# First layer of the last two token blocks by seven block products

## The chip, the cores and the metric

The kernel runs on one core of a Trainium2 chip. The time is device microseconds (us) of one execution. Six parts of the core appear below: TensorE (PE) multiplies matrices into PSUM banks, VectorE (DVE) and ScalarE (ACT) do everything between two products, GpSimd (POOL) only clears a few tiles at the start, SyncE (SP) puts transfers into DMA queues, and the DMA engines move data between DRAM and the core's SBUF.

## What is computed

Attention in chunks (4 batches, 8 heads, 768 tokens, head dimension 64) gives 3072 tokens of 512 features, and two feed-forward networks follow:

```python
x = attention(q, k, v, mem_k, mem_v)       # 24 chunks of 32 per sequence; keys: 8 memory, 16 left, 32 own, 8 right
h = x @ w_in                               # (3072, 512) @ (512, 2048): "first layer"
g = np.maximum(0.01 * h, h)
y = g @ w_out                              # (3072, 2048) @ (2048, 512): "second layer"
a, b = y @ w_a, y @ w_b                    # (3072, 512) @ (512, 1536), twice: "third layer"
out = (a * b) @ w_out2                     # (3072, 1536) @ (1536, 512)
```

Every float32 operand X is used as two parts, X = hi + lo (hi is a rounding to the type float32r, lo the rest), and a product W·X becomes three matmuls: lo·hi + hi·lo + hi·hi.

## The kernel before

**Blocks.** The tokens are six blocks of 512 (`TB`), numbered 0 to 5. Attention is done in 24 units of 128 tokens, four to a block. A unit is a short pipeline: `a_scores` (32 small matmuls on TensorE), `a_soft1` and `a_soft2` (maximum, difference, exponential, sum, division: VectorE and one ScalarE operation), `a_turn` (16 transposes of 32 rows on VectorE, in block 0 on TensorE), `a_pv` (32 small matmuls), and `a_out` (ScalarE makes the hi part of x, VectorE the lo part).

**Items.** The first two layers run as items (bi, f): block bi, feature tile f of 16. An item is `mm1` (4 groups of 3 matmuls of 512 columns into a PSUM bank of `ps_h`; then ScalarE makes g and gh, VectorE gl) and `mm2` of the item two places back (`LAG`), 12 matmuls of 512 columns into the four banks `acc` of the block (`ps_a`). The attention unit of block bi+1 is spread over the items of block bi: scores at item f, softmax at f+1, transposes at f+2, values at f+3, with f = 2, 5, 8, 11 in blocks 1 to 4. So block 4 carries the attention of block 5, and block 5 carries none. When `mm2` has done f = 15, ScalarE copies the four banks into tiles `x2` (tag `z`, three buffers), and a DMA writes each to the scratch tensor `x2d`.

**Preparation.** The weights of the third layer and of the last one are made ready by `prep_steps`: 18 groups of 4 steps. Steps one and two each join a raw weight tile (ACT one operation, DVE two), step three splits the plain blocks and makes four differences, step four splits those; the results go to DRAM. The loop over items takes 72 steps over the 64 items of blocks 1 to 4.

**The third layer** takes two blocks of 512 tokens at a time (`NS` = 3 pairs) as a 2 by 2 block product done with seven products in place of eight: `xc_make` builds the seven right-hand sides from the two x blocks with four subtractions (`t1` to `t4`), `layer3` runs the seven products.

**Order.** Tile's planner puts each engine's instructions in order by program position and by what its costs say is ready. `InOrder` is a wrapper around an engine: while `on` is true, each instruction that it emits is held behind the one that it emitted before on that engine, so the order is that of the program. It is on in the first items and from the third layer on; in the items between it is off, and the planner may run preparation ahead of its place.

**Queues.** Loads and stores are issued by SP, one after another: weights of the second layer (`wo_load`, tag `wo`, six buffers), attention inputs (`q_load`, `k_load`, `v_load`), raw weights, preparation's results, `x2d`, and `xs_load` (the x blocks of the third layer).

Of the kernel before, what the change touches and what calls it, by code (L numbers as in the profile page):

```python
# [14 lines left out]
P = 128  # L15
# [12 lines left out]
NB3 = NT // TB  # L28

# [24 lines left out]
def kernel(  # L54
# [74 lines left out]
    class Weights:  # L129
# [66 lines left out]

    att = tc.tile_pool(name="att", bufs=4, side="left")
# [4 lines left out]
        ap_.tile([P, 2 * CH, 16], F32, tag=t, name="qs", bufs=1) for t in ("pz", "ps", "pwa", "pwb")  # L202
# [18 lines left out]
    kt, vt, st, qr = {}, {}, {}, {}  # L221

    loaded = [0, 0, 0]

    def q_load(upto):
        while loaded[0] < min(upto, NU):
            u = loaded[0]
            if u < len(qs):
                eng = act if u < 1 else sp
                sp.dma_start(out=qs[u][0:64, 0:CH, :], in_=q_l[u, 0:64])  # L230
                eng.dma_start(out=qs[u][64:128, CH:2 * CH, :], in_=q_l[u, 64:128])
            else:
                t = ap_.tile([P, CH, 16], F32, tag="qr", name="qr", bufs=2)
                sp.dma_start(out=t, in_=q_l[u])
# [14 lines left out]
    def k_load(upto):  # L249
        while loaded[1] < min(upto, 2 * NU):  # L250
            u, cp = divmod(loaded[1], 2)
            t = ap_.tile([P, 512], F32, tag="k", name="k")
            sp.dma_start(out=t, in_=k_l[u, cp])
# [137 lines left out]
    x1 = {}  # L391

# [167 lines left out]
    for bi in range(1, NB3):  # L560
# [112 lines left out]
    def prep_steps():  # L676
        n = 0
        for p in range(NF2 // 2):
            for m in range(3):
# [17 lines left out]
                def plain(c, n, src):  # L697
                    w_parts(
                        wa[:, c:c + n, 0], wa[:, c:c + n, 1],
                        src.rearrange("p (a n) -> p a n", n=256), nc.vector,  # L700
                    )

                def plain4(c, src):
                    w_parts(*[
                        wa[:, c, l].rearrange("p (d a j) -> p d a j", d=2, j=32) for l in range(2)
                    ], src, nc.vector)

                def comb(c, x, y, op):
# [7 lines left out]
                    nc.vector.tensor_tensor(out=o, in0=x, in1=y, op=op)  # L716
# [25 lines left out]
                w_parts(wb[:, :, 0], wb[:, :, 1], t, nc.vector)  # L742
# [618 lines left out]
```

## Time and profile before

| | us |
|---|---|
| median of 3 runs | 1129.55 |
| lowest and highest | 1129.17, 1130.9 |
| the profiled execution | 1128.36 |
| its span, first to last instruction | 1126.5 |

The profile holds one execution. Its span is 1.9 us shorter than its time. Busy time of TensorE is that of pipelined matmuls whose ends are modelled: a matmul of 512 columns is listed with 389 ns, but the next one starts 227 ns after it, and the second number is what it costs in a row of them. The same holds in a smaller measure for VectorE and ScalarE, where independent operations overlap by some 80 to 100 ns.

### The profile page before, as it was taken

To read this page: it belongs to the slowest core of one execution; us is meant where nothing else is said; L and a number is where in the kernel's file an instruction comes from. 1 tells how busy PE (TensorE), PEld (TensorE's weight loads), DVE (VectorE), ACT (ScalarE), POOL (GpSimd) and SP (SyncE) were. 2 spreads that over 40 slices of the span, in tenths; PEclk is the share of its full clock that TensorE was granted. 3 is DMA by queue.
4 is the path that set the end of the run, shared out by engine and by line. 5 is a ranking of instruction groups with operands and counts; after the bars stand their busy time and mean duration, and the time that the engine had idled before them with its cause. 6 is when DMAs were issued, how large, how long until landed. Compare 5 with 4: busy or idle time off the path is not lost.

```text
span 1126.5 us, 16314 instructions
## 1 busy us (share of the span) xinstructions
PE 1108.6 (98%) x6242; PEld 919.2 (82%) x6242; DVE 726.6 (64%) x1334; ACT 499.4 (44%) x846; POOL 6.3 (1%) x16
## 2 busy tenths in 40 slices
PE   7899999999999999999999999999999999999997
PEld 6788888888888888888888888888888888888886
DVE  6796488778958873646111636578745679745666
ACT  5887555456555543425222434243434243343232
POOL 2000000000000000000000000000000000000000
PEclk9999999999999999999999999999999999999999
DMA  9996799999999985425445857566867576757452
GB/s 319 396 345 229 288 313 333 322 333 332 330 315 337 332 319 186 150 81 203 142 155 170 301 174 213 169 211 201 271 222 235 154 239 187 238 177 243 145 188 74
DMA packets 98509, 269.57 MB, mean 239 GB/s; under 512 B 9600, under 2 KB 23040, under 8 KB 97664
## 3 DMA queue, kind: packets, MB, share of 16 engines
q1 hardware_dynamic: 97264, 267.88, 71.0%
q8 instruction: 49, 0.80, 0.3%
q10 hardware_dynamic: 1168, 0.66, 0.2%
q14 instruction: 28, 0.23, 0.1%
HBM read 214.50 MB, written 54.00 MB: 238 GB/s over the span
## 4 chain that ended last, share of the span: by engine, by line
PE 97%; ACT 1%; DVE 1%; DMA 0%; SPq 0%; issue 0%; DVEq 0%
PE ca L47 18%; PE cc L47 9%; PE oa L47 8%; PE h L410 8%; PE a L530 8%; PE a L533 8%; PE a L534 8%; PE h L411 8%; PE h L412 8%; PE cb L47 5%; PE oy L47 4%; PE pv L383 2%; PE s L274 2%; PE oz L47 1%; ACT p L47 0%; DMA k<-kl 0%
## 5 line engine op out<-in xcount | busy, mean ns | idle before, releaser
L47 PE MATMUL ca<-ch,wab 128*128 128x512 f32 x575 | 191.8, 389 | 0.0
L410 PE MATMUL h<-xh,w 128*128 128x512 f32 (+1 forms) x384 | 151.5, 394 | 0.7 <-ACT xh L47 0.7
L530 PE MATMUL a<-gh,w 128*128 128x512 f32 (+1 forms) x392 | 150.6, 384 | 0.0
L533 PE MATMUL a<-gl,w 128*128 128x512 f32 (+1 forms) x392 | 150.4, 384 | 0.0
L534 PE MATMUL a<-gh,w 128*128 128x512 f32 (+1 forms) x392 | 150.4, 384 | 0.0
L411 PE MATMUL h<-xl,w 128*128 128x512 f32 (+1 forms) x384 | 148.5, 387 | 0.2 <-DVE xl L47 0.2
L412 PE MATMUL h<-xh,w 128*128 128x512 f32 (+1 forms) x384 | 148.4, 387 | 0.0
L508 DVE TENSOR_TENSOR gl<-g,gh 128x512 fp32r<-128x512 f32 (+1 forms) x96 | 65.3, 680 | 104.8 <-ACT gh L505 100.9
L47 ACT CAST st<-gb 128x512 fp32r<-128x512 f32 x126 | 76.5, 621 | 124.6 <-DVE gb L47 124.0
L47 PEld LDWEIGHTS ca<-ch,wab 128*128 128x128 f32 x575 | 107.9, 188 | 22.8
L502 ACT ACTIVATE g<-h 128x512 f32<-128x512 f32 (+1 forms) x96 | 56.3, 587 | 128.1 <-PE h L412 127.4
L47 PE MATMUL ca<-cl,wab 128*128 128x512 f32 x288 | 112.1, 389 | 0.0
L47 PE MATMUL oa<-st,wt 128*128 128x512 f32 x420 | 104.3, 389 | 0.0
L47 PE MATMUL cc<-ch,wab 128*128 128x512 f32 x288 | 100.4, 389 | 0.0
L47 DVE TENSOR_TENSOR st<-gb,st 128x512 fp32r<-128x512 f32 x126 | 85.3, 689 | 14.9 <-ACT st L47 13.2
L47 PEld LDWEIGHTS oa<-st,wt 128*128 128x128 f32 x420 | 78.8, 188 | 16.4
L530 PEld LDWEIGHTS a<-gh,w 128*128 128x128 f32 x392 | 73.7, 188 | 15.1 <-ACT x L547 0.4
L533 PEld LDWEIGHTS a<-gl,w 128*128 128x128 f32 x392 | 73.7, 188 | 14.5
L534 PEld LDWEIGHTS a<-gh,w 128*128 128x128 f32 x392 | 73.6, 188 | 14.5
L410 PEld LDWEIGHTS h<-xh,w 128*128 128x128 f32 x384 | 72.1, 188 | 16.3 <-ACT xh L47 0.8
L412 PEld LDWEIGHTS h<-xh,w 128*128 128x128 f32 x384 | 72.1, 188 | 14.7
L411 PEld LDWEIGHTS h<-xl,w 128*128 128x128 f32 x384 | 72.2, 188 | 14.2 <-DVE xl L47 0.5
(150 smaller groups left out, 1620.4 us busy)
## 6 DMA issues: line engine op xcount, KB each, us to landing
wab<-wab SPq DMA_DIRECT2D x126, 512.0 KB, 4.4
w<-wod SPq DMA_DIRECT2D x80, 512.0 KB, 5.0
raw<-w SPq DMA_DIRECT2D x68, 512.0 KB, 6.9
wt<-wtd SPq DMA_DIRECT2D x63, 512.0 KB, 4.5
k<-kl SPq DMA_DIRECT2D x48, 256.0 KB, 5.5
v<-vl SPq DMA_DIRECT2D x48, 256.0 KB, 5.2
wab<-pwb SPq DMA_DIRECT2D x12, 768.0 KB, 6.9
wod<-w SPq DMA_DIRECT2D x16, 512.0 KB, 6.3
```

The source lines that it names most:

```text
L47: self.last = emit(*args, **kwargs).ins
L274: pe.matmul(s[64 * cpar:64 * cpar + 64, cp * 4 + hp, :], qb[:, o, :], k[:, r:r + 64], start=True, stop=True,)
L383: pe.matmul(o[64 * hpar:64 * hpar + 64, 2 * pair:2 * pair + 2, t0:t0 + CH], v[:, i:i + 64], pt[:, 2 * cp + pair, 2 * cpar + hpar].rearrang ...
L410: pe.matmul(ps, w[1], x[0], start=first, stop=False)
L411: pe.matmul(ps, w[0], x[1], start=False, stop=False)
L412: pe.matmul(ps, w[0], x[0], start=False, stop=last)
L502: act.activation(g[:, c], ps[:, c], AF.Prelu, alpha=0.01)
L508: dve.tensor_tensor(out=gl[:, c], in0=g[:, c], in1=gh[:, c].bitcast(F32), op=ALU.subtract)
L530: pe.matmul(ps, slot[:, 1, c], gh[:, t], start=f == 0 and o == 0, stop=False, **kw)
L533: pe.matmul(ps, slot[:, 0, c], gl[:, t], start=False, stop=False, **kw)
L534: pe.matmul(ps, slot[:, 0, c], gh[:, t], start=False, stop=f == NF1 - 1 or (o == HALF and f == LEAD - 1), **kw)
```

## The change

Blocks 4 and 5 no longer run as items of their own. The first layer of both together is done as a 2 by 2 block product with seven products, per pair of feature tiles.

- **Attention.** 16 units (8 to 23) now lie beside the 48 items of blocks 1 to 3, started at the items in `STARTS`, two or three items apart instead of three, and five or more at a block's start; the last one starts at item 59 and its values come at item 62 of 63. `SEQ` puts unit 16 ahead of unit 12. Units of blocks 4 and 5 are written by `a_raw` as plain float32 into the tiles `xr` (ScalarE copy, no VectorE work); the first two go through DRAM (`x4d`), since the tile is not free yet.
- **Preparation.** 58 of the 72 steps lie in blocks 1 to 3. The other 14 lie in the new loop, two per pair.
- **Right-hand sides.** After block 3's items, `y_part` and `y_sub` build the seven right-hand sides Y from `xr`, with seven casts on ScalarE and eleven operations of 1024 columns on VectorE.
- **Seven products.** For each of 8 pairs of feature tiles, `s_sums` and `s_parts` build the four sums of W_in blocks, `prod` runs seven products of six matmuls, `snapped` and `summed` combine them, and `relu` makes g. The products of the second layer for block 4 run between them; the g of block 5 is kept in the freed W_in tiles (`kept`).
- **Output products of block 5** run last, 16 times 12 matmuls, in banks of `ps_h` and `ps_s`. `xs_load(0)` and `xc_make(0)` move there.
- `InOrder` is switched on ahead of `y_part(0)` for TensorE, VectorE and ScalarE, and stays on.

```diff
+NL = NB3 - 2
+SEQ = list(range(12)) + [16, 12, 13, 14, 15] + list(range(17, NU))
...
-                    raw = ap_.tile([P, 512, 2], I32, tag="raw", name="raw", bufs=4)
+                    raw = prep.tile([P, 512, 2], I32, tag="raw", name="raw", bufs=4)
...
+    prep_pool = tc.tile_pool(name="prep", bufs=1, side="left")
+    prep = prep_pool.__enter__()
...
+    qu, ku, vu = [[a[u] for u in SEQ] for a in (q_l, k_l, v_l)]
...
+    xr, x4d = {}, {}
+    def a_raw(u):
+        blk, k = divmod(SEQ[u], TB // UT)
+        o = pvt.pop(u)
+        c = slice(k * UT, k * UT + UT)
+        if blk in xr:
+            act.copy(xr[blk][:, :, c], o)
+            return
+        t = tp.tile([P, KC, UT], F32, tag="t", name="x4")
+        act.copy(t, o)
+        x4d[k] = dp.tile([P, KC, UT], F32, tag=f"x4d{k}", name=f"x4d{k}")
+        sp.dma_start(out=x4d[k], in_=t)
+    def x_raw():
+        for h, tag in enumerate(("xh", "xl")):
+            xr[NL + h] = xp.tile([P, KC, TB], F32, tag=tag, name="xr")
+        for k in x4d:
+            sp.dma_start(out=xr[NL][:, :, k * UT:k * UT + UT], in_=x4d[k])
...
-            acc[bi] = [ps_a.tile([P, TB], F32, tag="a", name="a") for _ in range(KC)]
+            last = bi == NB3 - 1
+            acc[bi] = [
+                p.tile([P, TB], F32, tag=t, name="a")
+                for p, t in (((ps_h, "h"), (ps_s, "s")) * 2 if last else ((ps_a, "a"),) * KC)
+            ]
...
-    for bi in range(1, NB3):
+    for bi in range(1, NL):
...
-    for bi in range(NB3 - 1):
-        for k, f in enumerate([5, 8, 11, 14] if bi == 0 else [2, 5, 8, 11]):
-            u = (bi + 1) * (TB // UT) + k
-            at(bi, f, a_scores, u)
-            at(bi, f, load_qk, u)
-            at(bi, f, a_soft1, u)
-            at(bi, f + 1, a_soft2, u)
-            if bi == 0:
-                at(bi, f + 2, a_turn_pe, u, ps_s, "s")
-            else:
-                at(bi, f + 2, a_turn, u)
-            at(bi, f + 3, a_pv, u, ps_s, "s")
-            at(bi, f + 3, load_v, u)
-            at(bi, f + 3, a_out, u, ("x", bi + 1), k * UT)
-    prep = ap_
+    for k, f in enumerate([5, 8, 11, 14]):
+        u = TB // UT + k
+        at(0, f, a_scores, u)
+        at(0, f, load_qk, u)
+        at(0, f, a_soft1, u)
+        at(0, f + 1, a_soft2, u)
+        at(0, f + 2, a_turn_pe, u, ps_s, "s")
+        at(0, f + 3, a_pv, u, ps_s, "s")
+        at(0, f + 3, load_v, u)
+        at(0, f + 3, a_out, u, ("x", 1), k * UT)
+    def at_item(i, *args):
+        at(*divmod(i, NF1), *args)
+    STARTS = (17, 20, 23, 26, 29, 32, 34, 37, 40, 42, 45, 48, 50, 53, 56, 59)
+    for k, i in enumerate(STARTS):
+        u = 2 * TB // UT + k
+        blk, o = divmod(SEQ[u], TB // UT)
+        at_item(i, a_scores, u)
+        at_item(i, load_qk, u)
+        at_item(i, a_soft1, u)
+        at_item(i + 1, a_soft2, u)
+        at_item(i + 2, a_turn, u)
+        at_item(i + 3, a_pv, u, ps_s, "s")
+        at_item(i + 3, load_v, u)
+        if blk < NL:
+            at_item(i + 3, a_out, u, ("x", blk), o * UT)
+        else:
+            at_item(i + 3, a_raw, u)
...
+    STEPS = 58
     for bi, f, parts in items[LEAD:]:
-        first, last = bi == 0, bi == NB3 - 1
-        if last and f == 0:
-            for _ in steps:
-                pass
-            att.__exit__(None, None, None)
-            xq = ctx.enter_context(
-                tc.tile_pool(name="xq", bufs=1, side="left", reuse_waits="tile")
-            )
-        if f == 0 and not last and not first:
-            x_tiles(("x", bi + 1))
+        first = bi == 0
+        if f == 0 and not first:
+            if bi + 1 < NL:
+                x_tiles(("x", bi + 1))
+            else:
+                x_raw()
...
-            for _ in range(72 * (i + 1) // 64 - 72 * i // 64):
+            n = (NL - 1) * NF1
+            for _ in range(STEPS * (i + 1) // n - STEPS * i // n):
...
+    att.__exit__(None, None, None)
+    xa_pool = tc.tile_pool(name="xa", bufs=1, side="left", reuse_waits="tile")
+    xa = xa_pool.__enter__()
+    ya, hc, homes = {}, KC // 2, {}
+    two = "p k n -> p (k n)"
+    def y_home(i, l):
+        if i in (0, 1, 3):
+            return xa.tile([P, hc, TB], F32R, tag=f"y{i}{l}", name="y")
+        if i == 2:
+            return wop.tile([P, hc, TB], F32R, tag="wo", name="y")
+        if i == 6:
+            key, tag, h = 6, "xh", l
+        else:
+            key, tag, h = l, ("xh", "xl")[l], i - 4
+        if key not in homes:
+            homes[key] = xp.tile([P, 2, hc, TB], F32R, tag=tag, name="y")
+        return homes[key][:, h]
+    def y_part(i):
+        t = Y[i].rearrange(two)
+        hi, lo = [y_home(i, l) for l in range(2)]
+        ya[i] = hi, lo
+        hi, lo = hi.rearrange(two), lo.rearrange(two)
+        act.copy(hi, t)
+        dve.tensor_tensor(out=lo, in0=t, in1=hi.bitcast(F32), op=ALU.subtract)
+    b11, b21, b12, b22 = [
+        xr[NL + h][:, k * hc:k * hc + hc] for h in range(2) for k in range(2)
+    ]
+    Y = (b11, b21, b21, b12, b12, b11, b22)
+    def y_sub(out, x, y):
+        dve.tensor_tensor(out=out, in0=x, in1=y, op=ALU.subtract)
+    sums_, sw = {}, {}
+    def s_sums(p):
+        zs = []
+        for f in (2 * p, 2 * p + 1):
+            w = wslot[f, 0]
+            z = tp.tile([P, 512], F32, tag="z", name="zs", bufs=3)
+            dve.tensor_tensor(out=z, in0=w[:, 0].bitcast(F32), in1=w[:, 1].bitcast(F32), op=ALU.add)
+            zs += [z[:, 0:256], z[:, 256:512]]
+        z11, z12, z21, z22 = zs
+        t = [tp.tile([P, 2, 256], F32, tag="t", name="sc") for _ in range(2)]
+        for o, x, y, op in (
+            (t[0][:, 1], z21, z22, ALU.add),
+            (t[0][:, 0], t[0][:, 1], z11, ALU.subtract),
+            (t[1][:, 0], z11, z21, ALU.subtract),
+            (t[1][:, 1], z12, t[0][:, 0], ALU.subtract),
+        ):
+            dve.tensor_tensor(out=o, in0=x, in1=y, op=op)
+        sums_[p] = t
+    def s_parts(p, h):
+        t = sums_[p][h]
+        w = xa.tile([P, 2, 2, 256], F32R, tag="sw", name="sw", bufs=3)
+        act.copy(w[:, 0], t)
+        dve.tensor_tensor(out=w[:, 1], in0=t, in1=w[:, 0].bitcast(F32), op=ALU.subtract)
+        for k, n in enumerate(((2, 3), (4, 6))[h]):
+            sw[p, n] = w[:, :, k]
+    def prod(ps, p, n, i, first):
+        if n in (0, 1, 5):
+            w = wslot[2 * p + (n == 5), 0]
+            w = w[:, :, 0:256] if n == 0 else w[:, :, 256:512]
+        else:
+            w = sw.pop((p, n))
+        hi, lo = ya[i]
+        for kc in range(hc):
+            c = slice(kc * P, kc * P + P)
+            kw = dict(skip_group_check=True)
+            pe.matmul(ps, w[:, 1, c], hi[:, kc], start=first and kc == 0, stop=False, **kw)
+            pe.matmul(ps, w[:, 0, c], lo[:, kc], start=False, stop=False, **kw)
+            pe.matmul(ps, w[:, 0, c], hi[:, kc], start=False, stop=kc == hc - 1, **kw)
+    def relu(src, kept=None):
+        g = tp.tile([P, TB], F32, tag="t", name="g")
+        act.activation(g, src, AF.Prelu, alpha=0.01)
+        if kept is None:
+            gh = tp.tile([P, TB], F32R, tag="gh", name="gh", bufs=3)
+            gl = tp.tile([P, TB], F32R, tag="gl", name="gl", bufs=3)
+        else:
+            w = wp.tile([P, 2, TB], F32R, tag=f"wi{kept}", name="g5")
+            gh, gl = w[:, 0], w[:, 1]
+        act.copy(gh, g)
+        def low():
+            dve.tensor_tensor(out=gl, in0=g, in1=gh.bitcast(F32), op=ALU.subtract)
+            return gh, gl
+        return low
+    def snapped(ps):
+        t = tp.tile([P, TB], F32, tag="t", name="u")
+        act.copy(t, ps)
+        return t
+    def summed(x, y):
+        t = tp.tile([P, TB], F32, tag="z", name="s", bufs=3)
+        dve.tensor_tensor(out=t, in0=x, in1=y, op=ALU.add)
+        return t
+    done2 = [(NL - 1) * NF1 - LAG]
+    def next2(item):
+        mm2(*item)
+        done2[0] += 1
+        wo_load(done2[0] + (4 if done2[0] < NL * NF1 else 6))
+    for e in (pe, dve, act):
+        e.on, e.last = True, None
+    whole = slice(0, TB)
+    def part2(bi, f, g):
+        return bi, [(0, TB, f)], g
+    y_part(0)
+    y_part(1)
+    next2(behind.pop(0))
+    y_sub(b12, b12, b11)
+    y_part(3)
+    y_sub(b12, b22, b12)
+    s_sums(0)
+    s_parts(0, 0)
+    y_part(4)
+    y_sub(b11, b12, b11)
+    y_part(5)
+    s_parts(0, 1)
+    y_sub(b21, b21, b12)
+    y_part(2)
+    y_part(6)
+    kept, late = {}, None
+    for p in range(NF1 // 2):
+        f0, f1 = 2 * p, 2 * p + 1
+        A = ps_h.tile([P, TB], F32, tag="h", name="A")
+        prod(A, p, 0, 0, True)
+        Bk = ps_s.tile([P, TB], F32, tag="s", name="B")
+        if p:
+            act.copy(Bk, A)
+            low12 = relu(late, f1 - 2)
+        else:
+            a1 = snapped(A)
+        next2(behind.pop(0))
+        if p:
+            kept[f0 - 2] = low12()
+        prod(Bk, p, 1, 1, p == 0)
+        if p:
+            next(steps, None)
+        if p + 1 < NF1 // 2:
+            s_sums(p + 1)
+        low11 = relu(Bk if p else summed(a1, Bk))
+        g11 = low11()
+        prod(A, p, 2, 4, False)
+        u2 = snapped(A)
+        C = ps_s.tile([P, TB], F32, tag="s", name="C")
+        prod(C, p, 3, 3, True)
+        if p + 1 < NF1 // 2:
+            s_parts(p + 1, 0)
+            s_parts(p + 1, 1)
+        prod(A, p, 4, 5, False)
+        u3 = snapped(A)
+        s22 = summed(u3, C)
+        next2(part2(NL, f0, g11))
+        kept[f1] = relu(s22, f0)()
+        if p:
+            next(steps, None)
+        prod(A, p, 5, 2, False)
+        low21 = relu(A)
+        prod(C, p, 6, 6, False)
+        behind.append(part2(NL, f1, low21()))
+        late = summed(u2, C)
+    low12 = relu(late, f1)
+    next2(behind.pop(0))
+    kept[f0] = low12()
+    for _ in steps:
+        pass
+    xa_pool.__exit__(None, None, None)
+    prep_pool.__exit__(None, None, None)
+    xq = ctx.enter_context(
+        tc.tile_pool(name="xq", bufs=1, side="left", reuse_waits="tile")
+    )
+    for f in range(NF1):
+        next2(part2(NL + 1, f, kept[f]))
+        if f == 0:
+            xs_load(0)
+        if f == 3:
+            xc_make(0, "t1")
+        if 4 <= f < 11:
+            for i in CHAIN[f - 4]:
+                xc_make(0, i)
...
-    for it in behind:
-        mm2(*it)
     for p in reversed(psum1):
         p.__exit__(None, None, None)
+    ps_o = ctx.enter_context(
+        tc.tile_pool(name="ps_o", bufs=2, space=bass.MemoryType.PSUM, reuse_waits="tile")
+    )
     ps_c = ctx.enter_context(
         tc.tile_pool(name="ps_c", bufs=1, space=bass.MemoryType.PSUM, reuse_waits="tile")
-    )
-    ps_o = ctx.enter_context(
-        tc.tile_pool(name="ps_o", bufs=2, space=bass.MemoryType.PSUM, reuse_waits="tile")
     )
     WT = (0, 1, 6, 3, 4, 5, 2)
...
-    for e in (pe, dve, act):
-        e.on, e.last = True, None
```

## Rows read from the trace of the kernel before

**Rows 1.** The page, part 1: busy time, share of the span, instructions.
```profile
PE 1108.6 (98%) x6242; PEld 919.2 (82%) x6242; DVE 726.6 (64%) x1334; ACT 499.4 (44%) x846; POOL 6.3 (1%) x16
```

**Rows 2.** The page, part 4: chain that ended last, by engine.
```profile
PE 97%; ACT 1%; DVE 1%; DMA 0%; SPq 0%; issue 0%; DVEq 0%
```

**Rows 3.** Busy time by stretch: blocks 1 and 3, 4, 5; last DMA share, GB/s.
```profile
140.00:234.00 94.00, 94.00 (x631) 77.61 (x630) 77.02 (x176) 50.37 (x81) 0.00 (x0) 1.00 0.94 327
...
328.00:422.00 94.00, 94.00 (x630) 77.31 (x629) 74.72 (x174) 51.32 (x82) 0.00 (x0) 1.00 0.95 330
422.00:510.00 88.00, 88.00 (x605) 72.62 (x604) 43.46 (x107) 31.09 (x47) 0.00 (x0) 1.00 0.42 140
510.00:597.00 87.00, 87.00 (x386) 72.03 (x385) 24.04 (x27) 27.96 (x43) 0.00 (x0) 1.00 0.44 157
```

**Rows 4.** The chain in order of time, third layer: six matmuls of 512 columns.
```profile
605.91 1.36 PE cb L47 x6
```

**Rows 5.** Groups by form, ScalarE: count, busy us, mean ns of one.
```profile
L505 ACT CAST gh<-g 128x512 fp32r<-128x512 f32 x93 | 57.7, 620 | 2.6
L502 ACT ACTIVATE g<-h 128x512 f32<-128x512 f32 x93 | 55.2, 593 | 124.7 <-PE h L412 124.0
L547 ACT COPY x<-a 128x512 f32<-128x512 f32 x20 | 11.0, 589 | 8.3 <-PE a L534 4.9 <-PE h L412 1.7 <-DMA x2d<-x 1.5
L771 ACT CAST ch<-xs 128x1024 fp32r<-128x1024 f32 x7 | 7.2, 1052 | 5.7 <-DMA xs<-x2d 5.7
```

**Rows 6.** Groups by form, VectorE.
```profile
L343 DVE STREAM_TRANSPOSE pt<-p 32x128 f32<-32x128 f32 x256 | 77.5, 303 | 4.3
L508 DVE TENSOR_TENSOR gl<-g,gh 128x512 fp32r<-128x512 f32 x93 | 64.0, 689 | 97.9 <-ACT gh L505 94.0 <-PE a L533 3.3
L117 DVE SCALAR_TENSOR_TENSOR pz<-raw,pz 128x512 int32<-128x512 int32 x36 | 24.9, 692 | 1.1
L114 DVE TENSOR_SCALAR pz<-raw 128x512 int32<-128x512 int32 x36 | 15.2, 423 | 13.6 <-ACT raw L104 13.2
L716 DVE TENSOR_TENSOR ps<-pz 128x256 f32<-128x256 f32 x36 | 14.6, 418 | 0.3
L776 DVE TENSOR_TENSOR cl<-xs,ch 128x1024 fp32r<-128x1024 f32 x7 | 8.4, 1224 | 5.2 <-ACT ch L771 5.1
L788 DVE TENSOR_TENSOR xs<-xs 128x1024 f32<-128x1024 f32 x4 | 4.9, 1223 | 1.8 <-DMA xs<-x2d 1.7
```

**Rows 7.** Timeline of TensorE, block 4: start, duration (us).
```profile
504.93 0.39 PE L534 MATMUL a<-gh,w 128*128 128x512 f32 x1
505.25 1.15 PE L383 MATMUL pv<-pt,v 128*64 128x64 f32 x32
506.33 0.50 PE L410 MATMUL h<-xh,w 128*128 128x512 f32 x1
```

**Rows 8.** Timeline of ScalarE: after the values; in block 5.
```profile
506.45 0.59 ACT L396 CAST xh<-pv 128x512 fp32r<-128x512 f32 x1 [2.56 <-PE pv L383]
...
531.77 0.62 ACT L505 CAST gh<-g 128x512 fp32r<-128x512 f32 x1
```

**Rows 9.** Timeline of VectorE, block 5.
```profile
532.43 0.69 DVE L508 TENSOR_TENSOR gl<-g,gh 128x512 fp32r<-128x512 f32 x1 [0.48 <-ACT gh L505]
```

**Rows 10.** Transfers of the tile x2 to DRAM: issue to landing.
```profile
DMA to landing us min/median/max: 1.9/2.8/4.7
```

**Rows 11.** Timeline of TensorE at the kernel's start.
```profile
10.30 2.93 PE L47 MATMUL warm<-id 128*128 128x128 f32 x12
13.02 0.86 PE L47 MATMUL pT<-id,p 128*128 128x128 f32 x4
13.72 1.50 PE L47 MATMUL warm<-id 128*128 128x128 f32 x12
```

**Rows 12.** Busy time by stretch, the kernel's end: the column after POOL is TensorE's clock.
```profile
1116.00:1120.00 4.00, 3.70 (x20) 2.93 (x18) 3.96 (x8) 1.07 (x3) 0.00 (x0) 1.00 0.85 217
1120.00:1122.00 2.00, 0.00 (x0) 0.00 (x0) 0.16 (x1) 0.00 (x0) 0.00 (x0) 1.00 0.79 212
1122.00:1124.00 2.00, 0.00 (x0) 0.00 (x0) 0.00 (x0) 0.00 (x0) 0.00 (x0) 0.72 0.96 254
```

**Rows 13.** DMA issues in block 5: count, KB each, median us to landing.
```profile
xs<-x2d SPq DMA_DIRECT2D x2, 1024.0 KB, 6.3
```

More of the change, by code (lines that the diff above doesn't have):

```diff
@@ L201 @@
     qs = [
-        ap_.tile([P, 2 * CH, 16], F32, tag=t, name="qs", bufs=1) for t in ("pz", "ps", "pwa", "pwb")
+        prep.tile([P, 2 * CH, 16], F32, tag=t, name="qs", bufs=1) for t in ("pz", "ps", "pwa", "pwb")
     ]
@@ L229, in q_load @@
                 eng = act if u < 1 else sp
-                sp.dma_start(out=qs[u][0:64, 0:CH, :], in_=q_l[u, 0:64])
-                eng.dma_start(out=qs[u][64:128, CH:2 * CH, :], in_=q_l[u, 64:128])
+                sp.dma_start(out=qs[u][0:64, 0:CH, :], in_=qu[u][0:64])
+                eng.dma_start(out=qs[u][64:128, CH:2 * CH, :], in_=qu[u][64:128])
             else:
                 t = ap_.tile([P, CH, 16], F32, tag="qr", name="qr", bufs=2)
-                sp.dma_start(out=t, in_=q_l[u])
+                sp.dma_start(out=t, in_=qu[u])
                 qr[u] = t
@@ L252, in k_load @@
             t = ap_.tile([P, 512], F32, tag="k", name="k")
-            sp.dma_start(out=t, in_=k_l[u, cp])
+            sp.dma_start(out=t, in_=ku[u][cp])
             kt[u, cp] = t
@@ L260, in v_load @@
             t = ap_.tile([P, 512], F32, tag="v", name="v")
-            sp.dma_start(out=t, in_=v_l[u, cp])
+            sp.dma_start(out=t, in_=vu[u][cp])
             vt[u, cp] = t
@@ L318, in a_soft2 @@
         p = pt_[u]
-        if u % UPB == 0:
+        if SEQ[u] % UPB == 0:
             dve.memset(p[0:64, 0:4, 0:LEFT], 0.0)
-        if u % UPB == UPB - 1:
+        if SEQ[u] % UPB == UPB - 1:
             dve.memset(p[64:128, 4:8, WIN - RIGHT:WIN], 0.0)
@@ L699, in plain @@
                         wa[:, c:c + n, 0], wa[:, c:c + n, 1],
-                        src.rearrange("p (a n) -> p a n", n=256), nc.vector,
+                        src.rearrange("p (a n) -> p a n", n=256), dve,
                     )
@@ L705, in plain4 @@
                         wa[:, c, l].rearrange("p (d a j) -> p d a j", d=2, j=32) for l in range(2)
-                    ], src, nc.vector)
+                    ], src, dve)
                 def comb(c, x, y, op):
@@ L715, in comb @@
                         ]
-                    nc.vector.tensor_tensor(out=o, in0=x, in1=y, op=op)
+                    dve.tensor_tensor(out=o, in0=x, in1=y, op=op)
                 if m < 2:
@@ L849 @@
             prep_load(f - NF1 + 1)
-        if last:
-            if f == 2:
-                xs_load(0)
-                xc_make(0, "t1")
-            if 4 <= f < 11:
-                for i in CHAIN[f - 4]:
-                    xc_make(0, i)
+    att.__exit__(None, None, None)
[15 more added lines that the diff above has]
+        return homes[key][:, h]
@@ new lines @@
+    sums_, sw = {}, {}
[14 more added lines that the diff above has]
+        ):
+            dve.tensor_tensor(out=o, in0=x, in1=y, op=op)
+        sums_[p] = t
```

2 lines of the change are left out of this document (1 added, 1 removed).

## The prediction

> **What bounds the kernel now.** I read the shares first: TensorE is busy 98% of the span, VectorE 64%, ScalarE 44% [rows 1]. The chain that ended last says the same more sharply: 97% of it is TensorE [rows 2]. So the time is the sum of TensorE's instructions, plus whatever gaps it gets. Third come the stretches by block [rows 3]: TensorE has no idle time in blocks 1 to 5. VectorE is at 75 to 77 of 94 us in blocks 1 to 3 and at 43 of 88 and 24 of 87 in blocks 4 and 5; the DMA engines are at 0.94 to 0.95 and 330 GB/s in blocks 1 to 3 and at 0.42 to 0.44 after. So all of preparation runs ahead into blocks 1 to 3, and the end of the first two layers is where VectorE and the queues are free. Last I read durations [rows 4 to 6] and what one engine needs to follow another: ScalarE reads a PSUM result 0.05 us after the modelled end on TensorE (505.25 + 1.15, then 506.45 [rows 7, 8]); VectorE follows ScalarE by 0.04 us (531.77 + 0.62, then 532.43 [rows 8, 9]).
>
> **TensorE's work.** Six matmuls of 512 columns take 1.36 us, 0.227 each [rows 4]. For two feature tiles the first layer of blocks 4 and 5 was 2 x 2 x 12 = 48 matmuls; it becomes 7 x 6 = 42. Over 8 pairs 384 become 336: 48 fewer, **-10.9 us**. Attention and the output products keep their matmuls. This saving counts only where TensorE is not made to wait.
>
> **Blocks 1 to 3.** They now hold 16 units in place of 12 and 58 of 72 steps, 14.5 of 18 groups. Transfers: before, three blocks of 94 us at about 327 GB/s moved 92 MB [rows 3]. By sizes in the code the four extra units add 5 MB, `x4d` 1 MB, and some 2.5 groups less take away 7 MB: about the same 91 MB, in some 9 us more. VectorE: about 226 us before [rows 3]. A unit is 16 transposes of 0.303, five operations of 0.69 and some small ones, 8.9 us [rows 6]; eight of the 16 units no longer make a lo part: +30. A group of preparation is 2 x (0.42 + 0.69) + 1.1 + 4 x 0.42 + 1.22 = 6.2 us: -16. 240 of 291 us is 82%, as before. I cost this at nothing; without that cover (VectorE late for the transposes) each late unit would hold TensorE by the delay itself, up to some 3 us in all.
>
> **The start of the new stage.** Here the order is the program's on all three engines. Set 0 at the end of the last unit's values (item 62). TensorE then has `mm1` of item 63 and `mm2` of 61, 62 and 63 (2.72 each) with products 0 and 1 (1.36 each) between: at 13.7 it wants the third product. That one writes bank A again, so it waits for ScalarE's copy `a1`. On ScalarE `a1` stands behind all seven casts of Y, and the last casts wait for VectorE. The chain: copy of the values 0.59; nine operations of 1024 columns on VectorE, 1.22 each (lo of Y1, Y3, Y4, Y5, Y2, four subtractions): 11.0; casts of Y1, Y3, Y5, Y2, Y6 that nothing covers, 1.05 each: 5.3; between second subtraction and Y4's lo two sums of 0.69, two of 0.42, a cast 0.62 and Y4's cast 1.05: 3.9; one lo of W sums 0.69; `a1` 0.59; 17 hand-overs of 0.04: 0.7. Together 22.7 [rows 5, 6]. (Y6 lives where b11 and b21 were, so its cast waits for Y2's lo.) TensorE waits 9 us.
>
> Queued behind `a1` on ScalarE are the four copies of block 3's output. They use three `z` buffers, so the fourth waits until the first transfer has landed, 2.8 us [rows 10]: copies end at 23.3, 23.9, 24.5 and, after 26.1, at 26.7. `s_sums(1)` on VectorE needs the second and third buffer, free at about 26.7 and 27.3, and takes 3.1: 29.7. `summed(a1, Bk)` needs the fourth, free at 29.6: 30.4. Then ScalarE's Prelu and cast (0.59 + 0.62), and only then `u2` (0.59): 32.2. TensorE's fifth product overwrites A and waits for it; without waits it would start at 16.4. So the delay is 15.8 us. Independent VectorE operations overlap by 0.08 or so; I take **+15**. Bounds: with Y1's parts done before 0, full overlap and no waits for transfers about +9; with landings of 4.7 [rows 10] twice and Y0's parts late too, +20.
>
> **TensorE's clock.** It idles about 9 us and again 4 to 5 us. After the kernel's last matmul (before 1120) the granted clock was 1.00 to 1122 and 0.72 over the next 2 us, so it went to the lower level (1.2 GHz) in a few us of idling [rows 12]. At the start twelve matmuls took 2.93 us, the next twelve, 3.4 us later, 1.50 [rows 11]: after a pause the lower level holds for some us of work. The third and fourth product at half speed (2.7 us more) fit into the second wait; after it some 4 us of work at half speed cost **+2.0**. Bounds: 0 (clock kept) and +5. The Trainium skill, page "TensorE: Matmul & The Clock Gate", section "HAM oscillation — how this bites in real kernels", says that waits inside a kernel throttle the array again, once per wait. By that rule of the Trainium skill both waits count and the price would be the upper bound, +5 in place of +2; no row shows a wait of that length inside this kernel.
>
> **The pairs.** A pair is 66 matmuls, 15.0 us. VectorE has 2 + 4 combinations for the next sums (3.1), 8 more operations of 0.69 (5.5), and two steps (joining, J, 0.42 + 0.69; splitting and four differences, P, 0.69 + 5 x 0.42; the last split, W, 1.2; a pair has P and W, or J twice): 10.8 or 12.6 us, in a fixed order. From the pair's start: `late` gives Prelu, cast and lo until 4.1, P until 6.9, sums until 10.0, g11's lo 10.7 less some overlap; TensorE wants g11 at 9.5. So a pair with P loses about 0.6 us, one with J (8.8) nothing. ScalarE's copies have 1.4 us of cover each. Four pairs with P and W: **+2.4** (bounds 0 and +6).
>
> **The tail.** `mm2` of block 4's last tile waits for relu and lo after its product: **+0.8** (bounds 0 and 1.5). Then 16 times 2.72 us of output products run over `xs_load` (6.3 us [rows 13], 8.2 us ahead of `t1`) and over eleven VectorE operations of 1.22: hidden; uncovered, the load would cost its 6.3. The last 14 steps issue their transfers in a stage where the DMA engines were at 0.42 to 0.44 [rows 3]: hidden; `wo_load` keeps four buffers and three outputs ahead. The swap of `ps_o` and `ps_c` gives the third layer banks that are long free: nothing.
>
> **Sum.** -10.9 + 15 + 2.0 + 2.4 + 0.8 = +9.3, so the profiled execution's 1128.36 would be 1137.7, and the median of the runs, 1.2 above it, **1138.8 us**. Own range of this case: 1133 to 1144.
>
> **Rivals.**
> *Covered start (faster).* The planner may place the last unit's values ahead of its item, since the order is free there. Each item earlier takes 5.4 us off the start; from 1.4 items on (7.7 us) the saving wins. Two items earlier: -10.9 + 4 + 2.4 + 0.8 = -3.7, 1125.8 us. For it: VectorE has slack in that stretch once preparation is done. Against it: in block 4 of the trace, with VectorE half idle, the values still stand right behind the twelve matmuls of their item (504.93, then 505.25 [rows 7]).
> *Even.* The same chain at its lower bound with the clock kept: -10.9 + 9 + 1.5 = -0.4, 1129.2 us. For it: operations overlap in places, and the second transfer may land early (minimum 1.9 [rows 10]). Against: the order leaves hardly anything to overlap.
> *Preparation late (slower still).* Transfers in blocks 1 to 3 would run at 91 MB in 291 us, 313 GB/s, near the 330 seen [rows 3]. If one group is left over at block 3's end, its 6.2 us of VectorE stand ahead of the Y chain: 1145 us.
> *Clock twice.* The clock goes down in both waits and takes the upper bound's 10 us of work at half speed to come back: +3 on the sum, 1141.8 us. The 0.72 after the last matmul speaks for it, the first block's quick recovery (3.4 us between the two sets of twelve) against [rows 11, 12]. It is what the Trainium skill's page on TensorE's clock gate, named above, would give.
> That the change saves no matmuls is excluded by the count.
>
> **Chances.** Forecast 46%, covered start 22%, even 12%, clock twice 12%, preparation late 8%. About 0.2% (2.3 us) is what a measurement of this kernel can tell from no change. Faster by more: 0.22 (the covered start); within: 0.14 (even, and the edge of the forecast); slower: 0.64. Leaving out the covered start's lower half (some 12%) and most of the late preparation, the range is 1125 to 1144.
>
> **What would show it.** Matmuls of the first layer's blocks 4 and 5: 336, at 0.227 us. A gap of TensorE of about 9 us ahead of the third product, released by ScalarE's `a1`, and a second of 4 to 5 us ahead of the fifth, released by `u2`; ScalarE's fourth copy of block 3 held by a transfer. A clock below 1.00 in that stretch. In the pairs, waits of under 1 us for g11's lo in every second one. I am wrong if the values of the last unit come more than one item early, if the casts of Y run ahead of their place, or if the chain's operations overlap far more than they do in the rows.

## The result, and the profile after

The changed kernel takes **1146.37 us** (median of 4 runs, 1146.2 to 1146.52), the kernel before beside it 1129.36: ratio 1.015, interval 1.0132 to 1.0167, so 17 us slower. The forecast was 1138.8 with a range up to 1144: the sign was right, the size 7.6 us short. The profiled span went from 1126.5 to 1144.6 us, **+18.1** (the execution profiled before, 1128.36, was 1.0 us below that median).

The page after, parts 1 and 4 (they answer to [rows 1] and [rows 2]):

```profile
PE 1105.0 (97%) x6194; PEld 912.8 (80%) x6194; DVE 776.0 (68%) x1418; ACT 527.3 (46%) x893; POOL 6.3 (1%) x16
...
PE 92%; DVE 2%; ACT 2%; DMA 2%; issue 1%; SPq 0%; DVEq 0%; ACTq 0%
```

TensorE has exactly 48 matmuls fewer (6242 to 6194), but its busy time fell by 3.6 us and not by 10.9: some matmuls ran at the lower clock (the stretches below). And the chain is no longer 97% TensorE. Which waits took its place is in the waits of TensorE (total us, times, longest us):

```profile
PE A L49 <- ACT u L49: 14.1, 2, 9.1
PE ca L49 <- DMA wab<-wab: 6.3, 1, 6.3
```

Two places: the block products' bank A, and the first weights of the third layer. The groups by line show that the products themselves are as counted, 96 + 96 + 96 + 48 = 336, and that only those with `sw` in their operands have a mean above 389 ns:

```profile
L49 PE MATMUL A<-y,sw 128*128 128x512 f32 x96 | 27.2, 422 | 14.1 <-ACT u L49 14.1
L49 PE MATMUL C<-y,sw 128*128 128x512 f32 x96 | 25.5, 403 | 0.0
L49 PE MATMUL A<-y,w 128*128 128x512 f32 x96 | 24.4, 389 | 0.0
...
L49 PE MATMUL B<-y,w 128*128 128x512 f32 x48 | 12.2, 389 | 0.0
```

**Busy time by stretch** (PE, PEld, DVE, ACT, POOL, granted clock, DMA share, GB/s): first two of the stretches of blocks 1 to 3 [rows 3], then the start of the new stage, its two waits each with the work behind it, then the start of the third layer.

```profile
140.00:234.00 94.00, 93.67 (x684) 77.34 (x683) 82.87 (x197) 52.40 (x84) 0.00 (x0) 1.00 0.94 332
...
328.00:424.00 96.00, 96.00 (x720) 79.11 (x720) 70.42 (x166) 48.30 (x75) 0.00 (x0) 1.00 0.77 273
432.00:441.00 9.00, 0.45 (x2) 0.02 (x1) 5.65 (x6) 3.66 (x5) 0.00 (x0) 0.75 0.16 58
441.00:447.00 6.00, 5.40 (x12) 3.80 (x12) 1.57 (x2) 2.52 (x5) 0.00 (x0) 0.53 0.76 197
447.00:452.00 5.00, 0.01 (x1) 0.01 (x1) 3.58 (x8) 1.80 (x4) 0.00 (x0) 0.81 0.46 184
452.00:458.00 6.00, 6.00 (x16) 4.76 (x17) 2.55 (x5) 2.82 (x5) 0.00 (x0) 0.59 0.01 3
613.00:621.00 8.00, 1.66 (x7) 1.13 (x6) 0.00 (x0) 1.66 (x3) 0.00 (x0) 0.77 0.90 272
621.00:630.00 9.00, 9.00 (x34) 7.22 (x33) 0.70 (x2) 1.76 (x3) 0.00 (x0) 0.82 0.81 298
```

In blocks 1 to 3 VectorE has 6 us more work in the first stretch than before and less in the third, and TensorE idles 0.3 us in all: the four extra units cost their own matmuls only. The clock is below 1.00 in and behind each of the two waits at the start, and again at the third layer.

**The start, on TensorE** (start, duration, idle before and its releaser). The products stand in their order; the output products between them are left out:

```profile
426.84 1.52 PE L49 MATMUL A<-y,w 128*128 128x512 f32 x6
...
430.92 1.52 PE L49 MATMUL B<-y,w 128*128 128x512 f32 x6
441.53 2.93 PE L49 MATMUL A<-y,sw 128*128 128x512 f32 x6 [9.08 <-ACT u L49]
444.25 2.67 PE L49 MATMUL C<-y,sw 128*128 128x512 f32 x6
451.99 2.93 PE L49 MATMUL A<-y,sw 128*128 128x512 f32 x6 [5.06 <-ACT u L49]
...
458.51 1.52 PE L49 MATMUL A<-y,w 128*128 128x512 f32 x6
...
461.23 1.07 PE L49 MATMUL A<-y,w 128*128 128x512 f32 x4
```

**The same on ScalarE and VectorE**: both copies `u` that release the waits, and what stands ahead of each.

```profile
439.94 1.04 ACT L49 CAST y<-xr 128x1024 fp32r<-128x1024 f32 x1 [1.29 <-DVE y L49]
440.90 0.58 ACT L49 COPY u<-A 128x512 f32<-128x512 f32 x1
441.37 1.56 ACT L49 COPY x<-a 128x512 f32<-128x512 f32 x3
444.57 0.59 ACT L49 COPY x<-a 128x512 f32<-128x512 f32 x1 [1.63 <-DMA x2d<-x]
450.17 0.63 ACT L49 ACTIVATE g<-s 128x512 f32<-128x512 f32 x1 [5.01 <-DVE s L49]
...
451.36 0.58 ACT L49 COPY u<-A 128x512 f32<-128x512 f32 x1
```
```profile
446.65 1.29 DVE L49 TENSOR_TENSOR zs<-w 128x512 f32<-128x512 f32 x2 [4.40 <-DMA x2d<-x]
...
449.46 0.68 DVE L49 TENSOR_TENSOR s<-u,B 128x512 f32<-128x512 f32 x1
```

This is the chain that the prediction wrote down: the last cast of Y, then `a1` at 440.90; three copies of block 3, the fourth held by a transfer; `zs` of pair 1 held by another; the sum, Prelu, cast, and only then the second `u`. From the first product to pair 1 it is 461.23 - 426.84 = 34.39 us where 66 matmuls would take 14.96: 19.4 lost.

**The start of the third layer.** Issues on SyncE before (`x2d` is block 5's output on its way to DRAM, `wab` the third layer's weights), then after, then the chain after:

```profile
577.75 3.68 SPq L869 DMA_DIRECT2D wab<-wab x5
603.15 1.68 SPq L548 DMA_DIRECT2D x2d<-x x3
```
```profile
593.68 4.52 SPq L853 DMA_DIRECT2D w<-wod  x3
612.83 1.68 SPq L577 DMA_DIRECT2D x2d<-x  x3
614.56 0.46 SPq L1094 DMA_DIRECT2D wab<-wab  x1
```
```profile
613.57 0.59 ACT x L49
...
614.56 5.82 DMA wab<-wab
...
620.51 2.90 PE ca L49 x6
623.41 1.81 PE cb L49 x6
```

Before, the weights were asked for 25 us ahead of the stores, during block 5. After, SyncE's queue has them behind the stores, which wait for the last copies: issue at 614.56, landed at 620.4, and TensorE then starts with six matmuls in 2.90 us where they take 1.36. The prediction had nothing for this place.

### The profile page after: what moved, and what is told of

It is laid out like the page before. It is cut to its first block, busy times and chain, and to the rows that moved or that the text cites. A ratio compares the mean times of both kernels' runs of the same rounds, so it can differ in the third digit from the quotient of the medians.

```text
span 1144.6 us, 16319 instructions
## 1 busy us (share of the span) xinstructions
PE 1105.0 (97%) x6194; PEld 912.8 (80%) x6194; DVE 776.0 (68%) x1418; ACT 527.3 (46%) x893; POOL 6.3 (1%) x16
## 4 chain that ended last, share of the span: by engine, by line
PE 92%; DVE 2%; ACT 2%; DMA 2%; issue 1%; SPq 0%; DVEq 0%; ACTq 0%
PE ca L49 18%; PE cc L49 9%; PE oa L49 8%; PE a L49 8%; PE h L435 5%; PE a L559 5%; PE h L436 5%; PE h L437 5%; PE a L562 5%; PE a L563 5%; PE cb L49 5%; PE oy L49 4%; PE A L49 4%; PE pv L388 2%; PE s L279 2%; PE C L49 2%
## 5 line engine op out<-in xcount | busy, mean ns | idle before, releaser
L435 PE MATMUL h<-xh,w 128*128 128x512 f32 (+1 forms) x256 | 101.7, 397 | 0.7 <-ACT xh L49 0.7
L436 PE MATMUL h<-xl,w 128*128 128x512 f32 (+1 forms) x256 | 98.7, 386 | 0.2 <-DVE xl L49 0.2
L437 PE MATMUL h<-xh,w 128*128 128x512 f32 (+1 forms) x256 | 98.7, 385 | 0.0
L559 PE MATMUL a<-gh,w 128*128 128x512 f32 (+1 forms) x256 | 97.7, 382 | 0.3 <-ACT x L576 0.3
L562 PE MATMUL a<-gl,w 128*128 128x512 f32 (+1 forms) x256 | 97.5, 381 | 0.0
L563 PE MATMUL a<-gh,w 128*128 128x512 f32 (+1 forms) x256 | 97.4, 381 | 0.0
L348 DVE STREAM_TRANSPOSE pt<-p 32x128 f32<-32x128 f32 x256 | 77.4, 302 | 4.3
L49 PEld LDWEIGHTS ca<-cl,wab 128*128 128x128 f32 x288 | 54.3, 189 | 11.1
L49 PEld LDWEIGHTS cc<-ch,wab 128*128 128x128 f32 x288 | 54.1, 188 | 11.3
L435 PEld LDWEIGHTS h<-xh,w 128*128 128x128 f32 x256 | 48.1, 188 | 11.3 <-ACT xh L49 0.8
L559 PEld LDWEIGHTS a<-gh,w 128*128 128x128 f32 x256 | 48.1, 188 | 10.1 <-ACT x L576 0.8
L49 PE MATMUL cc<-cl,wab 128*128 128x512 f32 x144 | 56.0, 389 | 0.0
```

What stands on the lines that cost most here:

```text
L49: self.last = emit(*args, **kwargs).ins
L348: dve.transpose(out=pt[o0:o0 + 32, :, 2 * cpar + hpar, hpx, :], in_=p[i0:i0 + 32, hpx::2, 32 * b:32 * b + 32],)
L435: pe.matmul(ps, w[1], x[0], start=first, stop=False)
L436: pe.matmul(ps, w[0], x[1], start=False, stop=False)
L437: pe.matmul(ps, w[0], x[0], start=False, stop=last)
L559: pe.matmul(ps, slot[:, 1, c], gh[:, t], start=f == 0 and o == 0, stop=False, **kw)
```

## The experiments

All ratios are to the kernel before, run beside each experiment on the same chip; where a text says "less", it is less than the change's 1146.37 (+17.0 us). The kernel before had medians from 1128.33 to 1129.36 in these sets, so a difference of about 1 us says little by itself. The edits are against the changed kernel unless another is named; `...` marks lines left out.

**e1: the third layer's weights.** Block 5's stores go out on ScalarE's queue, so that nothing in SyncE's queue waits for them.

```diff
-                    sp.dma_start(out=x2d[bi][:, e, t], in_=y[:, t])
+                    eng = nc.scalar if bi == NB3 - 1 else sp
+                    eng.dma_start(out=x2d[bi][:, e, t], in_=y[:, t])
```

> The stores of block 5's four x2 tiles are issued from ScalarE's queue, so that SP's queue holds nothing between the last wo load and the first loads of third-layer weights (wab). Theory (the wab loads are late only because they stand behind the x2d stores in SP's queue): the 6.3 us wait of TensorE at the third layer's first product goes, and with it the 2.0 us that its slow matmuls cost: about 1138 us against 1146.4 of the changed kernel. Rival (the wab tiles lie on W_in tiles that still hold the kept g, so the loads cannot start before the last output product whatever the queue): the wait stays near 6 us, 1146 us.

Measured: 1138.7 us (ratio 1.0087, 1.0072 to 1.0102), 7.7 us less. SyncE now issues the weights from 598.12 on, and in the stretch into the third layer the granted clock stays at 1.00 and TensorE is busy for 7.95 of 8 us:

```profile
598.12 22.07 SPq L1095 DMA_DIRECT2D wab<-wab  x7
```
```profile
612.00:620.00 8.00, 7.95 (x36) 6.24 (x35) 0.69 (x1) 3.42 (x6) 0.00 (x0) 1.00 0.75 226
```

The profiled span is 8.2 us shorter than that of the change. So the wait, and with it the low clock, came from where the loads stood in the queue: the first of them could go at 598.12 at the latest, and in the change it went at 614.56, behind the stores. Why they stand there no run shows. By the code two things differ: these weights take the memory of the first layer's weights, in which the change keeps relu outputs of block 5, read by the last output products; and `wab_load(5)`, which was written ahead of the last output products and their stores, is written behind them in the change. Moving that call alone was not tried.

**e2: the first wait alone.** The first product and `a1` ahead of Y4's parts.

```diff
     s_parts(0, 0)
+    A0 = ps_h.tile([P, TB], F32, tag="h", name="A")
+    prod(A0, 0, 0, 0, True)
+    a1 = snapped(A0)
     y_part(4)
...
```

> Only the first product of pair 0 and its copy a1 move in the program, to ahead of y_part(4). Theory (u2 is what binds: four x2 copies, the next sums and relu stand ahead of it on ScalarE and VectorE): the 9.1 us wait ahead of the third product goes, the wait ahead of the fifth grows by nearly as much, and the time changes by -0.5 us (0 to -2), about 1146 us. Rival (a1's place costs its own 9 us): about 1137 us.

Measured: 1146.59 us (ratio 1.0161, 1.0144 to 1.0178): no gain. The first wait is gone and the second is as long as both were:

```profile
435.07 1.53 PE L49 MATMUL C<-y,sw 128*128 128x512 f32 x6
452.79 2.93 PE L49 MATMUL A<-y,sw 128*128 128x512 f32 x6 [16.20 <-ACT u L49]
```

The 9 us ahead of the third product cost nothing by themselves; `u2`, at the end of the chain, sets the time.

**e3: the clock alone.** 38 and 32 more matmuls of 512 columns, into a bank that nobody reads, in the two waits.

```diff
...
         g11 = low11()
+        if p == 0:
+            busy(38)
         prod(A, p, 2, 4, False)
...
+        if p == 0:
+            busy(32)
         prod(A, p, 4, 5, False)
```

> Adds 38 dummy matmuls of 512 columns on TensorE ahead of pair 0's third product and 32 ahead of its fifth, into a spare bank; they fill the two waits (8.6 and 7.3 us) and change no result. Theory (the lower clock after the waits costs time of its own): the granted clock stays 1.00 there, the stretch behind the second wait is 2.6 us shorter, about 1143.8 us. Rival (the slow matmuls fall into waits anyway): 1146.4 us, same.

Measured: 1144.89 us (ratio 1.0143, 1.0128 to 1.0158), 1.5 less where 2.6 were expected. The clock stayed at 1.00 through both waits:

```profile
441.00:447.00 6.00, 5.53 (x24) 4.42 (x24) 1.60 (x2) 2.63 (x6) 0.00 (x0) 1.00 0.74 191
447.00:452.00 5.00, 4.94 (x22) 3.75 (x20) 3.58 (x8) 1.76 (x4) 0.00 (x0) 1.00 0.47 190
```

The fifth product starts where it did (452.04, after 451.99), and the sixth, at 456.25, follows 4.2 us later in place of 6.5 (451.99 to 458.51): the low clock cost 2.3 us there, and the rest of the start is waiting. Pair 1 starts 2.3 earlier too (458.97, after 461.23); the trace shows this better than the time, whose 1.5 is near what two sets differ by.

**e4: another order of the same work.** Pair 0's products, copies and relus are written between the steps that make Y, block 3's copies are split 3 + 1, and the sums of pair 1 come after pair 0. Nothing is left out or added. The core of it:

```diff
...
+    prod(A, 0, 0, 0, True)
+    a1 = snapped(A)
     y_part(4)
     y_sub(b11, b12, b11)
     s_parts(0, 1)
+    prod(Bk, 0, 1, 1, True)
+    prod(A, 0, 2, 4, False)
+    prod(C, 0, 3, 3, True)
+    for e in range(3):
+        out3.pop(0)()
     y_part(5)
+    u2 = snapped(A)
+    out3.pop(0)()
+    prod(A, 0, 4, 5, False)
+    low11 = relu(summed(a1, Bk))
...
```

> Pair 0's products, copies and relus are written into the program between the steps that build Y, and the next pair's sums come after them; the same instructions, another order, the four x2 copies split three and one. Theory (the two waits come from the program's order, not from the amount of work on VectorE and ScalarE): about 3 us of waits stay of the 16.8 us of delay, and the clock stays up: -16 us, about 1130.5 us. Rival (the chain of casts, lo parts and differences itself is as long as the waits): the delay stays above 10 us, 1140 us or more.

Measured: 1135.97 us (ratio 1.0062, 1.0046 to 1.0079), 10.4 less where 16 were expected. From the first product to pair 1 it is 19.93 us (34.39 after), so 14.5 were won there; the third to fifth products now run without a wait above 0.3 us, and the granted clock is 1.00 from 425 to 480 us:

```profile
432.68 1.43 PE L50 MATMUL A<-y,sw 128*128 128x512 f32 x5 [0.19 <-DVE y L50]
...
436.16 1.45 PE L50 MATMUL A<-y,sw 128*128 128x512 f32 x5 [0.28 <-DVE y L50]
```

Pair 1 lost 3.3 us of it again: its weight sums, now late, are cast on ScalarE ahead of its own copy B (a wait of 0.8), and its lo part comes 1.8 late. This trace is that of a run of 1134.23 us at a mean granted clock of 0.996. Two of the four took 1137.4 and 1137.5 us at 0.993, so the clock did not stay up in every execution.

**e5: e4 and e1 together.**

> The order of e4_order and the queue of e1_wab_queue together. Theory (the two losses lie in different places and add): 1136.0 less 7.7, about 1128.3 us, even with the kernel before. Rival (removing one only moves the wait to the other): above 1132 us.

Measured: 1128.15 us (10 runs; before 1129.28 in 21; ratio 0.9993, 0.9984 to 1.0002). The two losses are separate and add: 10.4 + 7.7 = 18.1 were expected and 18.2 came. The time is that of the kernel before, so the saving of TensorE just pays for what is still lost.

**e6: values two items earlier.** The prediction's covered start, by the list of starts alone.

```diff
-    STARTS = (17, 20, 23, 26, 29, 32, 34, 37, 40, 42, 45, 48, 50, 53, 56, 59)
+    STARTS = (17, 20, 23, 26, 29, 32, 34, 37, 40, 42, 45, 47, 50, 52, 55, 57)
```

> The changed kernel with the last five attention units started one or two items earlier, the last at item 57 in place of 59; nothing else. Theory (what counts is how much of TensorE's work lies between the last unit's values and the third product): 10.9 us more cover, the wait ahead of the third product goes, one of about 5 us stays ahead of the fifth (behind the x2 transfers), 1132 to 1135 us. Rival (VectorE cannot take the units closer together, TensorE waits for their transposes): waits of the same size in block 3, above 1141 us.

Measured: 1140.44 us (ratio 1.0101, 1.0087 to 1.0115), 5.9 less where 11 to 14 were expected. The values came 9.1 us earlier on ScalarE (409.53, after 418.67), but the chain did not move as a whole: Y4's cast came 5.0 us earlier only (425.03, after 430.02). On ScalarE it stands behind the relu of block 3's last item, ahead of which the engine waits 4.2 us for that item's matmuls. By the code the cast could not go ahead of them either, since Y4's parts lie in the buffers of block 3's input, which those matmuls read. Which of the two would bind alone no run shows. Both waits are left, one of them longer:

```profile
436.56 2.35 PE L49 MATMUL A<-y,sw 128*128 128x512 f32 x6 [2.37 <-ACT u L49]
...
446.92 2.93 PE L49 MATMUL A<-y,sw 128*128 128x512 f32 x6 [5.75 <-ACT u L49]
```

**e7: e4, e1 and e6 together.**

> Order, queue and starts together. Theory: of the changed kernel's losses only the waits in the pairs and the tail stay (2 to 5 us), 1120 to 1124 us, faster than the kernel before by 5 us or more. Rival (the order of e4 was already covered by nothing but chain length, or new waits in block 3): 1127 us or more.

Measured: 1127.29 us (11 runs; ratio 0.9984, 0.9974 to 0.9995), above the 1120 to 1124 that was expected and where the rival had it. First product to pair 1: 18.28 us. Pair 1 lost 4.9 us, partly in a low clock that followed a stretch in which TensorE was busy 6.62 of 9 us. In e5's trace pair 1 has the same two waits (0.8 and 1.8) at a clock of 1.00 and loses 3.3, so the low clock is some 1.6 of the 4.9:

```profile
450.00:459.00 9.00, 6.62 (x28) 5.17 (x29) 7.89 (x19) 6.01 (x13) 0.00 (x0) 1.00 0.38 146
459.00:463.00 4.00, 4.00 (x12) 3.13 (x11) 2.40 (x4) 2.19 (x3) 0.00 (x0) 0.57 0.00 0
```

**e8: the copies of block 3 alone.** They get buffers of `gh` and `gl` in place of the three of `z`, so that neither the fourth copy nor pair 1's sums wait for a transfer.

```diff
-                    y = tp.tile([P, TB], F32, tag="z", name="x2", bufs=3)
+                    y = tp.tile(
+                        [P, TB], F32, tag=("gh", "gl")[e % 2] if bi == NL - 1 else "z", name="x2", bufs=3
+                    )
```

> The four x2 copies of block 3 use free gh and gl buffers in place of the three z buffers, so no copy and no sum waits for a transfer; order as in the changed kernel. Theory (4.4 us of the second wait is the wait for transfers): u2 comes some 4 us earlier, about 1142 us. Rival (the chain of sums and relu is as late without it): above 1145 us.

Measured: 1140.47 us (ratio 1.01, 1.0086 to 1.0114), 5.9 less. VectorE's sums start at 442.23 (446.65 after), and of the second wait 1.48 is left:

```profile
447.56 1.65 PE L49 MATMUL A<-y,sw 128*128 128x512 f32 x6 [1.48 <-ACT u L49]
```

Beyond the 4.4 us that the transfer held, the fifth product was over in 1.65 us in place of 2.93: the second low stretch went with the second wait (granted clock 1.00 from 447.5 to 452). Pair 1 starts 6.7 us earlier (454.52, after 461.23).

**e10: e8 and e1 together**, two of the change's lines altered.

> Only two lines of the change altered: block 5's stores on ScalarE's queue (alone 1138.7, -7.7) and block 3's copies in tiles of their own (alone 1140.5, -5.9). Theory (the late weights of the third layer and the wait ahead of the fifth product are separate places): the two add, 1132.8. Rival (they share something, such as SyncE's queue or the clock): over 1135.

Measured: 1132.05 us (6 runs; before 1128.33; ratio 1.0028, 1.0016 to 1.0039): 14.3 less, where the two alone make 13.6. They add.

**e9: e7 with what its trace showed.** Pair 1's weight sums are split after the relu of pair 0's last value, block 3's copies have the buffers of e8, the buffers for Y2's parts are taken before the output product of feature tile 0, and no preparation runs beside pair 1: its two steps run ahead of the stage. The first of the four edits, against e7:

```diff
     late = summed(u2, C)
     s_sums(1)
-    s_parts(1, 0)
-    s_parts(1, 1)
...
             kept[f0 - 2] = low12()
+        if p == 1:
+            s_parts(1, 0)
+            s_parts(1, 1)
...
```

> The combination of the pair 0 order, the last stores on ScalarE's queue and the earlier attention starts (1127.3 us), with four things moved: block 3's copies of the accumulator have tiles of their own, the two buffers of the sum behind the sixth product are taken before the output product of feature tile 0, the weight sums of pair 1 are split after the relu of pair 0's last value, and the weight preparation has two more steps ahead of the stage and none beside pair 1. The combination lost 18.3 us from the first product to pair 1 (nominal 15.0) and 4.9 in pair 1, of which 3.4 at a low clock. Theory (the order of work on ScalarE and VectorE is what is left): the wait of 2.3 ahead of the sum and most of pair 1's loss go, together 4 to 6: 1121.5 to 1123.5. Rival (the losses are the amount of work on ScalarE and VectorE in this stage, whatever its order): within 1 us of 1127.3.

Measured: **1123.35 us** (5 runs, 1122.23 to 1124.01; before 1128.33; ratio 0.9952, 0.9939 to 0.9966): faster than both kernels by more than a measurement's 0.2%. TensorE's waits in the stage, and the clock in the stretch from the first products into pair 1:

```profile
PE A L50 <- DVE y L50: 1.1, 1, 1.1
PE C L50 <- DVE y L50: 0.7, 1, 0.7
PE a L50 <- DVE gl L50: 0.5, 2, 0.2
```
```profile
425.00:445.00 20.00, 17.76 (x75) 13.53 (x74) 9.94 (x12) 10.88 (x17) 0.00 (x0) 1.00 0.30 106
445.00:450.00 5.00, 5.00 (x23) 4.09 (x23) 4.47 (x10) 3.08 (x7) 0.00 (x0) 1.00 0.59 210
```

Pair 1 takes its 14.98 us. The start is still 18.38 us, as in e7, so the copies' tiles and Y2's buffers won nothing more there; what e9 has over e7 is pair 1. Gone there are the wait ahead of copy B and that for the late lo part, as the first edit meant; none of the four was run by itself. (The 3.4 us that the expectation puts on e7's low clock is too much: by e5 it is some 1.6.)

## Why the prediction was right in sign and short in size

**The saving held.** 48 matmuls fewer at 0.227 us, -10.9 us. Blocks 1 to 3 took the extra units at no cost beyond their own matmuls, as costed.

**The start of the stage (+15): the mechanism was right, the size 2 us short.** The fifth product should follow the first by 36 matmuls, 8.2 us, at 435.0; it started at 451.99, **17.0** late, where the working gave 15.8 and 15 was taken. The waits were named with their releasers and their lengths: 9 foreseen and 9.08 seen, 4 to 5 foreseen and 5.06 seen. Up to `a1` the working held to 0.2 us: from the copy of the last values at 418.62 it gave 22.7, and `a1` ended 22.9 after. Of the 2.0 that were missing, 0.8 is what was taken off for overlap, and 1.2 is the transfer, taken at 2.8 us, the median of [rows 10]. The one that VectorE's sums waited for took 4.1, inside the 1.9 to 4.7 of those rows:

```profile
442.48 4.08 DMA x2d<-x
```

e8 shows what the waits for stores were worth, 5.9. e2 shows that only the second of TensorE's waits counts, as the working had it.

**The clock (+2.0): right.** Fifth to sixth product took 6.52 us for 18 matmuls (4.08): **2.4**, of which e3 got back 2.3. With the 17.0 that is the whole loss of the start, 19.4. It went down in both waits (0.75 from 432, 0.81 from 447) and was low in the work behind them (0.53 from 441, 0.59 from 452); the first fall cost nothing, since the second wait absorbed it. By the rule of the Trainium skill that the prediction weighed (page "TensorE: Matmul & The Clock Gate", section "HAM oscillation — how this bites in real kernels") waits inside a kernel throttle the array again, once per wait. This trace agrees with that for its waits of 9.1, 5.1 and, at the third layer's start, 6.3 us, but not with the 5 us that the prediction set beside that rule.

**The pairs (+2.4): too high.** They lost 1.1 of the 2.4 foreseen: from pair 1 on their starts lie 15.33, 14.96, 15.30, 14.96, 15.30 and 14.96 us apart, so three pairs, not four, lose some 0.35 each, not 0.6.

**The tail (+0.8): right** for the last output products, 0.7.

**The failed step** is the last part of the tail: "The swap of `ps_o` and `ps_c` gives the third layer banks that are long free: nothing." I looked for what the third layer needs among PSUM banks and the input (`xs_load`), and not among its weights. Their loads, 25 us ahead of the stores before, fell behind them in SyncE's queue, and those stores wait for the end of the stage; why they fell behind is open (e1). That cost 6.3 us of waiting and, by the first twelve matmuls of the layer, 2.90 + 1.81 - 2 x 1.36 = 2.0 for the clock: 8.3, of which e1 gave back 8.2 by its span and 7.7 by its median.

**The sum with the measured terms**: -10.9 + 17.0 + 2.4 + 1.1 + 0.7 + 6.3 + 2.0 = 18.6; the span grew by 18.1. Without the failed step it would be +10.3, near the forecast's +9.3, and e1, with that step mended, takes 1138.7 us. That this is the forecast of 1138.8 almost to the digit is luck: the start with its clock was 2.4 short, the pairs were 1.3 too high, and the kernel before was 0.6 lower beside e1.

**The rivals.** The covered start, taken as two items at 5.4 us each, would have given 5.9 and not 10.8 (e6): what the values' place moves is only part of the chain. In the change itself the values did not move: they stand behind their own item's matmuls. "Clock twice" was right about the clock going down in both waits and wrong about its price. "Even" is out: the start was late by 17.0 and not by its 9. Preparation was not late: from 404 us to the end of Y's parts VectorE has no instruction of it.

## What to carry to other kernels

When a change rearranges the end of a stage, look up where the next stage's first loads stand in their in-order queue: behind stores that wait for the stage's end they are late, though the load itself took only 5.8 us here. Where one engine waits on a serial chain of others, the last wait on the chain was the price here; removing an earlier one moved it (e2). And the same instructions in another order took 10.4 us off (e4), so before a saving in matmuls is given up, write the order in which its operands are made beside that in which they are used.

## What was not expected of the hardware

The clock went low without a long wait in e7: after 9 us in which TensorE was busy 6.62, with no wait above 1.8 us, it was granted 0.57 over the next 4 us. In e5, with the same longest wait, it stayed at 1.00 over the same stretch:

```profile
450.00:470.00 20.00, 17.34 (x76) 13.72 (x75) 15.09 (x30) 12.99 (x23) 0.00 (x0) 1.00 0.39 144
```

What tells the two apart stays open, and one trace of each can't settle it: over the ten runs of e5 the mean granted clock of the same program goes from 0.996 to 0.999. The landing of the transfer above, 4.1 us where the median was 2.8, is inside the range before; whether the load of 1 MB that was issued 0.9 us after it had a part in it, no run shows.
